# Scores, pooled scores and values by head: two row halves of the matrix engine, two banks, no zero blocks, and a new issue order

## The chip, the cores and the metric

The kernel runs on one core of a Trainium2 chip. The metric is the device time of one execution in microseconds. The core's engines are PE (TensorE: matmuls, and PEld for the loads of their stationary weights), DVE (VectorE), ACT (ScalarE), POOL (GpSimd) and SP (SyncE, which issues most DMAs here). Each has its own instruction queue and works through it in order; semaphores tie them together. SBUF is the working memory of 128 partitions, PSUM the memory of eight banks (128 partitions by 512 f32 each) into which PE writes.

## The reference, cut to what matters

Eight batches of eight heads, 576 tokens, 64 numbers a head. The attention has two parts that are added: a local one, in which each token sees the three before and the three behind it, and a pooled one, in which groups of four tokens are averaged (144 rows), attend to each other, and are repeated four times. A mixture of eight experts, one for each token, follows on the 4608 token rows.

```python
q_d = q.reshape(B, H, Sd, factor, D).mean(axis=3)      # k_d, v_d alike; factor 4
out_up = np.repeat(sm_attn(q_d, k_d, v_d), factor, axis=2)
mask = np.abs(pos[:, None] - pos[None, :]) < factor
scores = np.where(mask, scale * np.matmul(q, k.transpose(0, 1, 3, 2)), -1000000000.0)
...
out_local = np.matmul(attn, v)
x = (out_up + out_local).transpose(0, 2, 1, 3).reshape(B * S, H * D)
e_idx = np.argmax(x[do_compute] @ w_gate, axis=1)      # do_compute: x @ w_skip > 0
y[mask] = gate_w[mask, None] * (np.maximum(xc[mask] @ w1[e], 0.0) @ w2[e])
```

## The kernel before, in words

The attention comes first, then the experts. Attention works on 36 tiles of 128 tokens. A tile is four groups of 32 tokens (`QG`); a group's local attention looks at a window of 38 keys (`KW`). Heads go in four pairs. Q and K of a batch lie with the 64 numbers of both heads of a pair on the 128 partitions, heads interleaved (partitions 0, 2, 4 ... are the first head's, 1, 3, 5 ... the second's).

K (`KB`) has two blocks of columns, one for each head, and in the block of a head the other head's partitions are zero. So one matmul over 128 rows gives the scores of both heads of a pair beside each other. For the first two batches K comes with its zeros from memory (`load_kb`); later batches overwrite only the head's own partitions (`load_k`). The pooled K (`KD`, by `pool_k`) keeps that form, and so do the V windows (`VB`, by `load_v`, two DMAs of 48 rows a tile): 96 rows, interleaved by head, with zeros where row and block belong to different heads.

For a tile, `scores` writes the mask by an identity matmul in bf16, then 16 f32 matmuls (four pairs by four groups; a group's 32 tokens are one 32-column strip of the array, and of the partitions of the result). `s_max`, `s_sub`, `s_sum` (DVE), `s_exp` (ACT) and `norm` (POOL) make the probabilities `E`; `p_transpose` turns them through PE, `p_evac` copies them out of PSUM; `up_mm` starts the result `O` with the pooled attention repeated by a matmul with a 0/1 matrix (`rep`); `values` adds 16 f32 matmuls; `x_out` copies `O` to `X`, `store_x` writes it, and `x_transpose`, `x_evac`, `logits` prepare the routing. For a batch, `d_scores` (five a batch), `d_max`, `d_neg`, `d_exp`, `d_transpose`, `d_values`, `d_out`, `d_hi`, `d_lo` make the pooled attention `up` in a high and a low half. Routing (`route`) runs every eight tiles.

PSUM is in four pools of two banks each: `psS` for scores, `psD` for pooled scores and routing, `psT` for what is transposed, `psO` for results and logits.

The order on every engine is not the program's own: all steps are recorded as nodes, and the table `ORDER` (1262 numbers) says in which order they are issued on all engines and queues. Each engine then runs its part in order and waits for what its next instruction needs: data, or the release of a buffer of a pool.

The lines by which a step can be found in the profile of before: L252 and L249 `d_scores`, L241 `pool_k`, L257, L262, L273 the maximum, negation and exponential of pooled scores, L306 to L318 `d_values`, L335 `d_out`, L341 and L344 `d_hi` and `d_lo`, L352 the mask, L357 the scores, L362, L368, L374, L378 the softmax steps, L394 `p_transpose`, L398 `p_evac`, L413 `up_mm`, L419 `values`, L424 `x_out`, L433 `x_transpose`, L445 `logits`, L825 and L845 the two matmuls of the experts.

Of the kernel before, what the change touches and what calls it, by code (L numbers as in the profile page):

```python
# [108 lines left out]
)  # L109

@with_exitstack
def tile_attention_moe(ctx, tc, qT, kT, kB, vW, v4, vr, mask, cst, ups, cid, w9, w1, w2, out):
# [77 lines left out]
    def load_v(i):  # L193
        V = TT[i]["VB"] = VBs[i % 3]
        for r in range(2):
            nc.sync.dma_start(out=V[r::2, r].rearrange("p a g d -> p (a g d)"), in_=vW[i, r])
# [839 lines left out]
```

## Time and profile before

| | us |
|---|---|
| median of 3 runs (lowest to highest) | 506.4 (503.98 to 508.02) |
| the profiled execution's own time | 505.92 |
| its span, from first to last instruction | 504.1 |
| PE busy | 447.2 (89%) |
| PE weight loads busy | 381.8 (76%) |
| DVE busy | 316.3 (63%) |
| ACT busy | 242.8 (48%) |
| POOL busy | 167.8 (33%) |
| DMA | 101.50 MB, mean 201 GB/s |

Busy is the union of an engine's instructions, and the ends of matmuls are modelled, so how long PE is held by a piece of work is better read from the distance between starts. A row of grouped instructions has line, engine, operation, tiles (out<-in), shapes and count; behind the bar its busy time, the mean of one in ns, and the idle time of the engine just before, with what ended it. A row of the timeline has start, length, then the same and a count. A row of waits has who waited for whom, in total, how often, and the longest.

### The profile page before, as it was taken

What the parts mean: (1) busy time and instruction counts of PE and PEld (TensorE: products, weight loads), DVE (VectorE), ACT (ScalarE), POOL (GpSimd) and SP (SyncE); (2) the same over time, 40 slices, a digit from 0 to 9 for tenths busy, and PEclk for the clock granted to TensorE, in tenths of its full rate; (3) what the DMA queues carried; (4) which work ended last, traced back from release to release, by engine and by line L of the source; (5) the groups of instructions that cost most, each with busy time, mean ns of one, the idle gap of its engine ahead of it and who ended that gap; (6) DMA issues with size and microseconds to landing.
All of it is one profiled execution on the core that took longest, in us unless ns stands there. A gap on an engine that the chain in (4) does not pass through costs nothing. (4 is left out here: it accounts for less than half of the span.)

```text
span 504.1 us, 13771 instructions
## 1 busy us (share of the span) xinstructions
PE 447.2 (89%) x5642; PEld 381.8 (76%) x5642; DVE 316.3 (63%) x617; ACT 242.8 (48%) x558; POOL 167.8 (33%) x178
## 2 busy tenths in 40 slices
PE   0678899989997999998499999999999999999991
PEld 0346677767886778886389898989989889898981
DVE  1799689479967995625254655635676755567421
ACT  1356477637683677462244354335454534454310
POOL 7356667465736352110420040410505050201002
PEclk9999989999999999998589999999999999999996
DMA  7986996989899663451554555464666753555201
GB/s 271 356 282 194 304 340 212 305 275 312 233 303 338 213 199 108 158 164 60 181 177 126 169 194 168 136 225 134 231 218 238 238 190 121 177 192 169 84 4 56
DMA packets 34620, 101.50 MB, mean 201 GB/s; under 512 B 5069, under 2 KB 6349, under 8 KB 34530
## 3 DMA queue, kind: packets, MB, share of 16 engines
q1 hardware_dynamic: 30690, 89.14, 53.7%
q0 software_dynamic: 3840, 11.09, 6.2%
q8 instruction: 65, 1.06, 0.9%
q14 instruction: 25, 0.20, 0.1%
HBM read 85.98 MB, written 15.73 MB: 202 GB/s over the span
## 5 line engine op out<-in xcount | busy, mean ns | idle before, releaser
L794 POOL DMA_INDIRECT out<-Y,six x24 | 24.2, 1009 | 192.6 <-DVE Y L852 189.7
L825 PE MATMUL ph<-xth,w1h 128*128 128x384 f32 (+2 forms) x256 | 81.6, 319 | 0.7 <-issue 0.7
L825 PE MATMUL ph<-xtl,w1h 128*128 128x384 f32 (+2 forms) x256 | 79.8, 312 | 0.1
L825 PE MATMUL ph<-xth,w1l 128*128 128x384 f32 (+2 forms) x256 | 79.7, 311 | 0.0
L845 PE MATMUL py<-w2h,hh 128*128 128x512 f32 x168 | 65.8, 392 | 0.5
L845 PE MATMUL py<-w2l,hh 128*128 128x512 f32 x168 | 65.8, 392 | 0.0
L845 PE MATMUL py<-w2h,hl 128*128 128x512 f32 x168 | 65.6, 391 | 0.0
L834 ACT ACTIVATE hh<-ph 128x384 fp32r<-128x384 f32 x64 | 31.3, 491 | 58.3 <-PE ph L825 28.2
L835 DVE SCALAR_TENSOR_TENSOR hl<-ph,hh 128x384 fp32r<-128x384 f32 x64 | 34.7, 554 | 37.5 <-ACT hh L834 35.8
L825 PEld LDWEIGHTS ph<-xth,w1h 128*128 128x128 f32 x256 | 49.1, 192 | 1.5 <-issue 1.1
L825 PEld LDWEIGHTS ph<-xtl,w1h 128*128 128x128 f32 x256 | 49.0, 191 | 0.8 <-issue 0.4
L241 DVE TENSOR_REDUCE KD<-KB 128x288 f32<-128x1152 f32 x31 | 40.8, 1339 | 13.7 <-DMA KB<-kB 11.5
L825 PEld LDWEIGHTS ph<-xth,w1l 128*128 128x128 f32 x256 | 48.9, 191 | 0.0
L387 POOL TENSOR_TENSOR Et<-Et,r 128x304 f32<-128x304 f32 x36 | 25.9, 725 | 62.7 <-DVE r L384 36.6
L599 DVE TENSOR_TENSOR w2l<-raw,w2h 128x1024 fp32r<-128x1024 f32 x32 | 39.1, 1221 | 10.7 <-ACT w2h L598 10.5
L614 DVE TENSOR_TENSOR w1l<-raw,w1h 128x1024 fp32r<-128x1024 f32 x32 | 39.2, 1224 | 9.4 <-ACT w1h L609 9.4
L816 ACT CAST xth<-Tx 128x512 fp32r<-128x512 f32 x22 | 12.9, 587 | 62.7 <-PE Tx L813 59.3
L252 PE MATMUL Sd<-KD,qd 128*128 128x288 f32 x64 | 23.9, 470 | 19.2 <-DVE KD L241 16.6
L817 DVE TENSOR_TENSOR xtl<-Tx,xth 128x512 fp32r<-128x512 f32 x22 | 15.2, 692 | 40.5 <-ACT xth L816 37.2
L598 ACT CAST w2h<-raw 128x1024 fp32r<-128x1024 f32 x32 | 33.6, 1050 | 14.4 <-PE py L845 14.4
L419 PE MATMUL O<-VB,PT 96*32 96x128 f32 x1152 | 38.3, 274 | 0.0
L794 POOL DMA_INDIRECT xr<-out,gix x24 | 27.7, 1154 | 30.9 <-DMA raw<-w 23.8
(136 smaller groups left out, 962.4 us busy)
## 6 DMA issues: line engine op xcount, KB each, us to landing
raw<-w SPq DMA_DIRECT2D x64, 512.0 KB, 3.3
VB<-vW SPq DMA_DIRECT2D x72, 192.0 KB, 4.6
out<-X SPq DMA_DIRECT2D x36, 256.0 KB, 3.7
V<-v SPq DMA_DIRECT2D x16, 512.0 KB, 9.4
Q<-qT SPq DMA_DIRECT2D x7, 1152.0 KB, 8.8
KB<-kT SPq DMA_DIRECT2D x12, 576.0 KB, 9.3
KB<-kB SPq DMA_DIRECT2D x4, 832.0 KB, 7.1
KB<-kB SPq DMA_DIRECT2D x2, 768.0 KB
```

The lines of the kernel that those rows point to most:

```text
L241: nc.vector.tensor_reduce(out=kd, in_=kv, axis=AX.X, op=ALU.add)
L252: nc.tensor.matmul(pairs(S), lhsT=B[b]["qd"][:, n, :128], rhs=kd[:, :, n, :], start=True, stop=True)
L387: nc.gpsimd.tensor_tensor(out=TT[i]["E"], in0=TT[i]["E"], in1=heads(TT[i]["r"])[:, :, None, :].to_broadcast([128, 4, KW, 2]), op=ALU.mult)
L419: nc.tensor.matmul(O[quad[j], 128 * a:128 * a + 128], lhsT=PT[:, a, quad[j]], rhs=VB[:, :, a, j, :], start=False, stop=a == 3)
L598: nc.scalar.copy(out=hf, in_=raw)
L599: nc.vector.tensor_tensor(out=flat(lo), in0=raw, in1=hf.bitcast(F32), op=ALU.subtract)
L614: nc.vector.tensor_tensor(out=flat(lo), in0=raws[e, j], in1=flat(hi).bitcast(F32), op=ALU.subtract)
L794: ins = nc.gpsimd.indirect_dma_start(bounds_check=NOUT - 1, oob_is_err=False, **kw).ins
L825: nc.tensor.matmul(P[i][:, :n], lhsT=a[:, c, 128 * i:128 * i + 128], rhs=bb[:, c, :n], start=m == 0, stop=m == 11)
L834: nc.scalar.activation(out=hh[:, i], in_=p, func=AF.Relu)
L835: nc.vector.scalar_tensor_tensor(out=hl[:, i], in0=p, scalar=0.0, in1=hh[:, i].bitcast(F32), op0=ALU.max, op1=ALU.subtract)
L845: nc.tensor.matmul(py[k], lhsT=a[:, i, ks], rhs=bb[:, i, :], start=(j == 0 and i == 0 and m == 0), stop=(j == 3 and i == 1 and m == 2))
```

## The change

Each head is now worked by itself over its own rows. Q, K and their pooled forms have a pair's first head on partitions 0 to 63 and the second on 64 to 127; the zero blocks and the loads of them are gone (`KB` and `KD` are half as wide, and only three columns at each end of K are filled with zeros). A pair's two heads are two matmuls, one in each row half of the array, and their results go to two PSUM banks: `scores` has 32 f32 matmuls of 38 columns in place of 16 of 76 (and eight of the mask for four), `d_scores` two of 144 for one of 288, `values` 32 of 64 columns for 16 of 128. `values` takes 38 of each 64 rows; `KR` goes from 48 to 64, so a V window has 128 rows, is loaded by one DMA, and has four buffers in place of three.

PSUM: a tile of `psS` is two banks and is shared by scores, pooled scores and routing (two buffers); `psO` is one buffer of two banks, for results alone; `d_values` and `logits` take a buffer of `psT`. `up_mm` writes each 512-column step as two of 256; for the last 64 tokens of a batch it has one step for both halves of `up`, where it had four of 128 columns, and for that `d_out` spreads the rest rows over 512 columns (`d_spread_r`, and `up` is 1024 wide, before 640).

```diff
-KR = 48
+KR = 64
-NREP = R_REST + 4 * 192
+NREP = R_REST + 192
...
     psS = pool(att, "psS", 2, space=PSUM)
-    psD = pool(att, "psD", 2, space=PSUM)
     psT = pool(att, "psT", 2, space=PSUM)
-    psO = pool(att, "psO", 2, space=PSUM)
+    psO = pool(att, "psO", 1, space=PSUM)
...
-    KBs = [kvp.tile([128, 2, KF], F32, name=f"KB{i}") for i in range(2)]
-    VBs = [kvp.tile([WV, 2, 4, 4, HD], F32, name=f"VB{i}") for i in range(3)]
-    Es = [kvp.tile([128, 4, KR, 2], F32, name=f"Et{i}") for i in range(3)]
+    KBs = [kvp.tile([128, KF], F32, name=f"KB{i}") for i in range(2)]
+    VBs = [kvp.tile([WV, 4, 4, HD], F32, name=f"VB{i}") for i in range(4)]
+    Es = [kvp.tile([128, H, KR], F32, name=f"Et{i}") for i in range(3)]
...
-    halves = [slice(0, 128, 2), slice(1, 128, 2)]
+    halves = [slice(0, 64), slice(64, 128)]
...
-        V = TT[i]["VB"] = VBs[i % 3]
-        for r in range(2):
-            nc.sync.dma_start(out=V[r::2, r].rearrange("p a g d -> p (a g d)"), in_=vW[i, r])
+        V = TT[i]["VB"] = VBs[i % 4]
+        nc.sync.dma_start(out=V.rearrange("p a g d -> p (a g d)"), in_=vW[i])
...
     def pool_k(b, p):
-        kd, o = KDs[b % 2][:, :, p, :], KO + SEQ * p
-        kv = KBs[b % 2][:, :, o:o + SEQ].rearrange("p h (i r) -> p h i r", r=4)
-        if b == 0 and p == 1:
-            for r in range(3):
-                nc.gpsimd.tensor_add(out=kd, in0=kv[:, :, :, 0] if r == 0 else kd, in1=kv[:, :, :, r + 1])
-        else:
-            nc.vector.tensor_reduce(out=kd, in_=kv, axis=AX.X, op=ALU.add)
+        kd, o = KDs[b % 2][:, p, :], KO + SEQ * p
+        kv = KBs[b % 2][:, o:o + SEQ].rearrange("p (i r) -> p i r", r=4)
+        nc.vector.tensor_reduce(out=kd, in_=kv, axis=AX.X, op=ALU.add)
...
     def d_scores(b, n):
-        S = psD.tile([128, 512], F32, name="Sd")
...
-            nc.tensor.matmul(pairs(S), lhsT=B[b]["qd"][:, n, :128], rhs=kd[:, :, n, :], start=True, stop=True)
...
+        S = psS.tile([128, 2, 512], F32, name="S")
+        Sv, kd, qd = S[:, :, :SD], KDs[b % 2], B[b]["qd"]
+        for p in range(4) if n == 4 else (n,):
+            rows, q = (quad[p], slice(SD - 32, SD)) if n == 4 else (slice(None), slice(0, 128))
+            for h, hs in enumerate(halves):
+                nc.tensor.matmul(Sv[rows, h], lhsT=qd[hs, p, q], rhs=kd[hs, p], start=True, stop=True)
...
+    def d_spread_r(b):
+        r = B[b]["rm"] = smp.tile([128, 4, 2], F32, name="rm", bufs=2)
+        nc.vector.tensor_tensor(out=r, in0=B[b]["rd", 1][:, None, :].to_broadcast([128, 4, 2]),
+                                in1=cs[:, C_SP4:C_SP4 + 4][:, :, None].to_broadcast([128, 4, 2]), op=ALU.mult)
...
         for p in range(4):
             for j, b, g in groups(i):
                 o, k = SEQ * p + QG * g, KO + SEQ * p + QG * g - 3
-                nc.tensor.matmul(Sv[quad[j], 2 * p:2 * p + 2], lhsT=B[b]["Q"][:, o:o + QG],
-                                 rhs=KBs[b % 2][:, :, k:k + KW], start=False, stop=p == 3)
+                for h, hs in enumerate(halves):
+                    nc.tensor.matmul(Sv[quad[j], h, p], lhsT=B[b]["Q"][hs, o:o + QG], rhs=KBs[b % 2][hs, k:k + KW],
+                                     start=False, stop=p == 3)
...
     def up_mm(i):
-        O = TT[i]["O"] = psO.tile([128, 512], F32, name="O")
...
+        for n, (l, u) in enumerate(steps):
+            for h in range(2):
+                nc.tensor.matmul(O[:, h], lhsT=l, rhs=u.rearrange("p (a h d) -> p h a d", a=4, h=2)[:, h],
+                                 start=n == 0, stop=False)
...
         for a in range(4):
             for j in range(4):
-                nc.tensor.matmul(O[quad[j], 128 * a:128 * a + 128], lhsT=PT[:, a, quad[j]], rhs=VB[:, :, a, j, :],
-                                 start=False, stop=a == 3)
+                for h in range(2):
+                    rows = slice(KR * h, KR * h + KW)
+                    nc.tensor.matmul(O[quad[j], h, a], lhsT=PT[rows, a, quad[j]], rhs=VB[rows, a, j],
+                                     start=False, stop=a == 3)
...
-        Lp = LP[i0] = psO.tile([128, 512], F32, name="O")
+        Lp = LP[i0] = psT.tile([128, 512], F32, name="T")
```

`ORDER` is a new table. On PE, at the first tiles, before (L413 is `up_mm`, L419 `values`, L252 a pooled score, L433 and L394 the transposes; the numbers tell buffers of one name apart):

```order
L413 MATMUL O_487<-upH_470,rep_120 128x512
L413 MATMUL O_487<-upL_471,rep_120 128x512
L413 MATMUL O_490<-upH_470,rep_120 128x512
L413 MATMUL O_490<-upL_471,rep_120 128x512
L419 MATMUL O_487<-VB0_114,PT_474 32x128 x16
L252 MATMUL Sd_519<-KD1_122,qd_455 128x288
L433 MATMUL T_522<-ident_69,X_517 128x128 x4
```

The same place with the change (L421 is `values`, L412 `up_mm`, L435 the x transpose, L239 a pooled score):

```order
L421 MATMUL O_607<-VB0_111,PT_553 32x64 x32
L412 MATMUL O_708<-upH_543,rep_118 128x256 x2
L412 MATMUL O_708<-upL_544,rep_118 128x256 x2
L435 MATMUL T_717<-ident_69,X_700 128x128 x4
L239 MATMUL S_724<-KD1_120,qd_533 128x144 x2
L239 MATMUL S_732<-KD1_120,qd_533 128x144 x2
L421 MATMUL O_708<-VB1_112,PT_557 32x64 x32
```

Two results were begun ahead of the first `values`; now the second `up_mm` stands behind the first `values`, with nothing between them, and can only start once `O_607` is copied out.

On PE around the tiles 7 and 8, before (the second `values` is tile 8's; it is also one of the tiles with last rows of a batch, hence the matmuls of 128 columns):

```order
L419 MATMUL O_1363<-VB1_115,PT_1182 32x128 x16
L433 MATMUL T_1425<-ident_69,X_1311 128x128 x4
L394 MATMUL T_1436<-ident_69,Et0_117 96x128 x4
L413 MATMUL O_1445<-upH_938,rep_120 128x512
L413 MATMUL O_1445<-upL_939,rep_120 128x512
L413 MATMUL O_1445<-upH_938,rep_120 128x128 x4
L413 MATMUL O_1445<-upL_939,rep_120 128x128 x4
L433 MATMUL T_1463<-ident_69,X_1430 128x128 x4
L419 MATMUL O_1445<-VB2_116,PT_1270 32x128 x16
```

With the change, around the tiles 8 and 9 (L392 is `p_transpose`):

```order
L421 MATMUL O_1806<-VB0_111,PT_1788 32x64 x32
L392 MATMUL T_1900<-ident_69,Et1_116 128x128 x4
L435 MATMUL T_1909<-ident_69,X_1795 128x128 x4
L412 MATMUL O_1916<-upH_1741,rep_118 128x256 x2
L412 MATMUL O_1916<-upL_1742,rep_118 128x256 x2
L435 MATMUL T_1927<-ident_69,X_1905 128x128 x4
L239 MATMUL S_1935<-KD1_120,qd_1751 128x144 x2
L421 MATMUL O_1916<-VB1_112,PT_1815 32x64 x32
L239 MATMUL S_1978<-KD1_120,qd_1751 128x144 x2
```

Between a tile's `values` and the next `up_mm` stand a transpose of probabilities and one of x, as before. The pooled scores of a batch now stand close to each other between the steps of the tiles, and take the buffers `S` that the scores take too.

More of the change, by code (lines that the diff above doesn't have):

```diff
@@ L41, with tile_attention_moe @@
 R_REST = 64 + SEQ
-NREP = R_REST + 4 * 192
+NREP = R_REST + 192
 BIG = float(1 << 20)
 ORDER = (
[61 rows of a table removed]
[61 rows of a table added]
 )
 @with_exitstack
-def tile_attention_moe(ctx, tc, qT, kT, kB, vW, v4, vr, mask, cst, ups, cid, w9, w1, w2, out):
+def tile_attention_moe(ctx, tc, qT, kT, vW, v4, vr, mask, cst, ups, cid, w9, w1, w2, out):
     nc = tc.nc
@@ L154, in tile_attention_moe @@
     ones = kvp.tile([128, 128], BF16, name="ones")
-    KBs = [kvp.tile([128, 2, KF], F32, name=f"KB{i}") for i in range(2)]
-    VBs = [kvp.tile([WV, 2, 4, 4, HD], F32, name=f"VB{i}") for i in range(3)]
-    Es = [kvp.tile([128, 4, KR, 2], F32, name=f"Et{i}") for i in range(3)]
+    KBs = [kvp.tile([128, KF], F32, name=f"KB{i}") for i in range(2)]
+    VBs = [kvp.tile([WV, 4, 4, HD], F32, name=f"VB{i}") for i in range(4)]
+    Es = [kvp.tile([128, H, KR], F32, name=f"Et{i}") for i in range(3)]
     rep = kvp.tile([128, NREP], F32R, name="rep")
-    KDs = [kvp.tile([128, 2, 4, SD], F32, name=f"KD{i}") for i in range(2)]
-    halves = [slice(0, 128, 2), slice(1, 128, 2)]
+    KDs = [kvp.tile([128, 4, SD], F32, name=f"KD{i}") for i in range(2)]
+    halves = [slice(0, 64), slice(64, 128)]
     flat = lambda a: a.rearrange("p a b -> p (a b)")
@@ L175, in load_q, with load_k @@
         nc.sync.dma_start(out=chunk(B[b]["Q"])[:, c], in_=qT[b, c].rearrange("c p n -> p c n"))
[L177 to L183 removed]
+    def load_k(b, c=slice(None)):
+        nc.sync.dma_start(out=chunk(KBs[b % 2][:, KO:KO + 4 * SEQ])[:, c], in_=kT[b, c].rearrange("c p n -> p c n"))
     def load_v4(b, k):
@@ L234, in pool_k @@
     def pool_k(b, p):
-        kd, o = KDs[b % 2][:, :, p, :], KO + SEQ * p
-        kv = KBs[b % 2][:, :, o:o + SEQ].rearrange("p h (i r) -> p h i r", r=4)
-        if b == 0 and p == 1:
-            for r in range(3):
-                nc.gpsimd.tensor_add(out=kd, in0=kv[:, :, :, 0] if r == 0 else kd, in1=kv[:, :, :, r + 1])
-        else:
-            nc.vector.tensor_reduce(out=kd, in_=kv, axis=AX.X, op=ALU.add)
-    def d_scores(b, n):
-        S = psD.tile([128, 512], F32, name="Sd")
-        pairs = lambda rows: rows[:, :2 * SD].rearrange("p (a k) -> p a k", a=2)
-        kd = KDs[b % 2]
-        if n == 4:
-            for p in range(4):
-                nc.tensor.matmul(pairs(S[32 * p:32 * p + 32]), lhsT=B[b]["qd"][:, p, SD - 32:], rhs=kd[:, :, p, :],
-                                 start=True, stop=True)
-        else:
-            nc.tensor.matmul(pairs(S), lhsT=B[b]["qd"][:, n, :128], rhs=kd[:, :, n, :], start=True, stop=True)
-        B[b]["Sd"][n] = pairs(S)
+        kd, o = KDs[b % 2][:, p, :], KO + SEQ * p
+        kv = KBs[b % 2][:, o:o + SEQ].rearrange("p (i r) -> p i r", r=4)
+        nc.vector.tensor_reduce(out=kd, in_=kv, axis=AX.X, op=ALU.add)
+    def d_scores(b, n):
+        S = psS.tile([128, 2, 512], F32, name="S")
[4 more added lines that the diff above has]
+                nc.tensor.matmul(Sv[rows, h], lhsT=qd[hs, p, q], rhs=kd[hs, p], start=True, stop=True)
+        B[b]["Sd"][n] = Sv
     def d_max(b, n):
@@ L301, in d_values @@
         s = B[b]
-        O = psO.tile([128, 512], F32, name="O")
+        O = psT.tile([128, 512], F32, name="T")
         PT, vd = s["PTd"], s["vd"]
@@ L334, in d_out @@
-        upS = s["upS"][:, D:] if c else s["upS"][:, :D]
-        nc.vector.scalar_tensor_tensor(out=upS.rearrange("p (h d) -> p h d", h=n),
-                                       in0=s["Od", c][:, :n * HD].rearrange("p (h d) -> p h d", h=n), scalar=0.25,
-                                       in1=s["rd", c][:, :, None].to_broadcast([128, n, HD]), op0=ALU.mult, op1=ALU.mult)
+            s["upS"] = dp.tile([128, 2, D], F32, name="upS", bufs=1)
+        if c == 0:
+            hd = lambda a: a.rearrange("p (h d) -> p h d", h=H)
+            o, r = hd(s["Od", 0]), s["rd", 0][:, :, None].to_broadcast([128, H, HD])
+        else:
+            hd = lambda a: a.rearrange("p (a h d) -> p a h d", a=4, h=2)
+            o = s["Od", 1][:, :128].rearrange("p (h d) -> p h d", h=2)[:, None].to_broadcast([128, 4, 2, HD])
+            r = s["rm"][:, :, :, None].to_broadcast([128, 4, 2, HD])
@@ L339, in d_hi @@
+        nc.vector.scalar_tensor_tensor(out=hd(s["upS"][:, c]), in0=o, scalar=0.25, in1=r, op0=ALU.mult, op1=ALU.mult)
     def d_hi(b):
-        B[b]["up"] = [dp.tile([128, D + 128], F32R, name="upH"), dp.tile([128, D + 128], F32R, name="upL")]
-        nc.scalar.copy(out=B[b]["up"][0], in_=B[b]["upS"])
+        B[b]["up"] = [dp.tile([128, 2, D], F32R, name="upH"), dp.tile([128, 2, D], F32R, name="upL")]
+        nc.scalar.copy(out=flat(B[b]["up"][0]), in_=flat(B[b]["upS"]))
     def d_lo(b):
-        nc.vector.tensor_tensor(out=B[b]["up"][1], in0=B[b]["upS"], in1=B[b]["up"][0].bitcast(F32), op=ALU.subtract)
+        nc.vector.tensor_tensor(out=flat(B[b]["up"][1]), in0=flat(B[b]["upS"]), in1=flat(B[b]["up"][0]).bitcast(F32),
+                                op=ALU.subtract)
@@ L347, in scores @@
     def scores(i):
-        S = psS.tile([128, 512], F32, name="S")
-        Sv = TT[i]["S"] = S[:, :H * KW].rearrange("p (h k) -> p h k", h=H)
+        S = psS.tile([128, 2, 512], F32, name="S")
+        Sv = TT[i]["S"] = S[:, :, :4 * KW].rearrange("p h (a k) -> p h a k", a=4)
         for j, b, g in groups(i):
             v = 0 if g == 0 else (2 if g == NG - 1 else 1)
-            nc.tensor.matmul(Sv[quad[j]], lhsT=idb[:, quad[j]], rhs=mk[:, v:v + 1, :].to_broadcast([128, H, KW]),
-                             start=True, stop=False)
+            for h, hs in enumerate(halves):
+                o = 64 * h + 32 * (j % 2)
+                nc.tensor.matmul(Sv[quad[j], h], lhsT=idb[hs, o:o + 32], rhs=mk[hs, v:v + 1, :].to_broadcast([64, 4, KW]),
+                                 start=True, stop=False)
@@ L401, in up_mm @@
     def up_mm(i):
-        O = TT[i]["O"] = psO.tile([128, 512], F32, name="O")
-        main, rest = [], []
+        O = psO.tile([128, 2, 512], F32, name="O")
+        O = TT[i]["O"] = O[:, :, :4 * HD].rearrange("p h (a d) -> p h a d", a=4)
+        steps = []
         for b in sorted({b for j, b, g in groups(i)}):
             o = 128 * i - SEQ * b
-            if o < 4 * 128:
-                main += [(O, rep[:, 64 + o:192 + o], u[:, :D]) for u in B[b]["up"]]
-            if o + 128 > 4 * 128:
-                r = R_REST + o - 448
-                rest += [(O[:, 128 * p:128 * p + 128], rep[:, r + 192 * p:r + 192 * p + 128], u[:, D:])
-                         for u in B[b]["up"] for p in range(4)]
-        for n, (o, l, u) in enumerate(main + rest):
-            nc.tensor.matmul(o, lhsT=l, rhs=u, start=n == 0, stop=False)
+            for u in B[b]["up"]:
+                if o < 4 * 128:
+                    steps.append((rep[:, 64 + o:192 + o], u[:, 0]))
+                if o + 128 > 4 * 128:
+                    steps.append((rep[:, R_REST + o - 448:R_REST + o - 320], u[:, 1]))
+        for n, (l, u) in enumerate(steps):
+            for h in range(2):
+                nc.tensor.matmul(O[:, h], lhsT=l, rhs=u.rearrange("p (a h d) -> p h a d", a=4, h=2)[:, h],
+                                 start=n == 0, stop=False)
     def values(i):
@@ L468, in bank @@
         def bank(name):
-            R[name] = psD.tile([128, 512], F32, name="Sd")
+            R[name] = psS.tile([128, 2, 512], F32, name="S")[:, 0]
             return R[name]
@@ L636, in load_zrow @@
     def load_zrow():
-        nc.sync.dma_start(out=out[0:1, :], in_=VBs[0][0:1, 1, :2].rearrange("p a g d -> p (a g d)"))
+        nc.sync.dma_start(out=out[0:1, :], in_=flat(Es[2])[0:1])
     node(load, mkf, mask)
@@ L642, in tile_attention_moe @@
         node(load_q, 0, slice(c, c + 1))
-        node(load_kb, 0, c)
+        node(load_k, 0, slice(c, c + 1))
+    for i in range(2):
+        for o in (KO - 3, KO + 4 * SEQ):
+            node(fill, nc.vector, KBs[i][:, o:o + 3])
     node(copy, nc.vector, idb, ident)
     node(copy, nc.vector, mk, mkf)
-    node(fill, nc.gpsimd, VBs[0])
     node(fill, nc.gpsimd, Es[0])
@@ L649, in tile_attention_moe @@
     node(load, cs, cst)
-    reps = slice(0, R_REST), slice(R_REST, NREP)
-    repf = [rawp.tile([128, 1024], F32, name="raw")[:, :c.stop - c.start] for c in reps]
-    for r, c in enumerate(reps):
-        node(load, repf[r], ups[:, c])
+    repf = rawp.tile([128, 1024], F32, name="raw")[:, :NREP]
+    node(load, repf, ups)
     for j in range(2):
@@ L659, in tile_attention_moe @@
     node(load, w9t, w9)
+    for i in range(1, 3):
+        node(fill, nc.gpsimd, Es[i])
     node(load_zrow)
-    for i in range(1, 3):
-        node(fill, nc.gpsimd, VBs[i])
-        node(fill, nc.gpsimd, Es[i])
     node(fill, nc.gpsimd, ones, 1.0)
     node(copy, nc.vector, tri, cs[:, C_TRI:C_TRI + 128])
-    for r, c in enumerate(reps):
-        node(copy, nc.scalar, rep[:, c], repf[r])
+    node(copy, nc.scalar, rep, repf)
     node(copy, nc.vector, BT, cs[:, C_BASE:C_BASE + E + 1])
@@ L671, in tile_attention_moe @@
             node(load_q, b)
-            for c in range(3) if b == 1 else ():
-                node(load_kb, b, c)
-            for hh in range(2) if b > 1 else ():
-                node(load_k, b, hh)
+            node(load_k, b)
             for j in range(3):
@@ L972, in layouts @@
     f32 = np.float32
-    pair = lambda a: np.ascontiguousarray(a.reshape(B, 4, 2, SEQ, HD).transpose(0, 4, 2, 1, 3)).reshape(B, 128, 4, SEQ)
+    pair = lambda a: np.ascontiguousarray(a.reshape(B, 4, 2, SEQ, HD).transpose(0, 2, 4, 1, 3)).reshape(B, 128, 4, SEQ)
     chunks = lambda a: np.ascontiguousarray(a.reshape(B, 128, 3, CH).transpose(0, 2, 1, 3))
     qT, kT = chunks(pair(q)), chunks(pair(k))
-    kB = np.zeros((2, 128, 2, KF), f32)
-    for h in range(2):
-        kB[:, h::2, h, KO:KO + 4 * SEQ] = pair(k)[:2, h::2].reshape(2, 64, 4 * SEQ)
     vp = np.zeros((B, H, QG * (NG - 1) + KR, HD), f32)
@@ L1011, in layouts @@
     ups[:, :R_REST] = tok[None] // 4 == row[:, None]
-    for p in range(4):
-        for t in range(64):
-            ups[32 * p + 16 + t // 4, R_REST + 192 * p + 64 + t] = 1.0
+    for t in range(64):
+        ups[16 + t // 4::32, R_REST + 64 + t] = 1.0
     w9 = np.concatenate([moe_w_gate, moe_w_skip[:, None]], axis=1)
@@ L1021, in layouts @@
     w2 = np.ascontiguousarray(w2).reshape(E, 4, 128, 1024)
-    return dict(qT=qT, kT=kT, kB=kB, vW=vW, v4=v4, vr=vr, mask=mask, cst=cst, ups=ups, cid=cid, w9=w9, w1=w1, w2=w2)
+    return dict(qT=qT, kT=kT, vW=vW, v4=v4, vr=vr, mask=mask, cst=cst, ups=ups, cid=cid, w9=w9, w1=w1, w2=w2)
 def kernel(q, k, v, moe_w_skip, moe_w_gate, moe_w1, moe_w2):
```

35 lines of the change are left out of this document (14 added, 21 removed), and 122 rows, old and new, of the table ORDER.

## The prediction

> **What bounds the kernel now.** I first split the span into stages, with each engine's busy time, the share of the DMA engines that was busy, and GB/s.
>
> ```profile
> core 0: us, PE busy (x) PEld busy (x) DVE busy (x) ACT busy (x) POOL busy (x), PEclk, DMA share, GB/s
> 0.00:16.60 16.60, 0.00 (x0) 0.03 (x1) 3.71 (x4) 1.28 (x1) 10.32 (x21) 1.00 0.84 302
> 16.60:50.00 33.40, 27.22 (x522) 18.66 (x522) 30.40 (x66) 19.48 (x68) 18.63 (x22) 1.00 0.81 261
> 50.00:175.00 125.00, 112.61 (x2427) 89.91 (x2424) 99.75 (x231) 77.64 (x236) 72.68 (x71) 0.99 0.88 282
> 175.00:230.00 55.00, 55.00 (x1236) 46.32 (x1239) 32.66 (x95) 35.04 (x94) 14.25 (x19) 1.00 0.48 159
> 242.00:504.00 262.00, 243.90 (x1371) 219.58 (x1371) 141.27 (x178) 106.63 (x155) 51.90 (x48) 0.96 0.49 165
> ```
>
> The attention fills the first 230 us, then comes a routing tail to 242 and the expert half, which the change doesn't touch: those 262 us stay. Before 16.6 PE waits for data; up to 50 VectorE is the fullest (30.4 of 33.4); from 50 to 175 PE leads (112.6 of 125), with DMA close behind (0.88); from 175 to 230 PE has no gap at all. So a shorter PE pays whole only at the end. The start:
>
> ```profile
> 15.10 1.35 DVE L241 TENSOR_REDUCE KD<-KB 128x288 f32<-128x1152 f32 x1 [11.54 <-DMA KB<-kB]
> ```
>
> The first K must land (15.1) and be pooled before PE has work. Next, PE in one piece of its timeline (start, length, records; a new group's start ends the turn of the one before):
>
> ```profile
> 130.89 0.32 PE L352 MATMUL S<-mk,idb 128*32 128x304 bf16 x4
> 131.03 0.70 PE L357 MATMUL S<-KB,Q 128*32 128x76 f32 x32
> 131.56 1.05 PE L419 MATMUL O<-VB,PT 96*32 96x128 f32 x32
> 132.44 1.03 PE L306 MATMUL O<-vb,PTd 128*32 128x512 f32 x8
> 133.30 1.06 PE L309 MATMUL O<-vd,PTd 128*32 128x64 f32 x64
> 134.19 0.39 PE L313 MATMUL O<-vb,PTd 128*32 128x128 f32 x8
> 134.73 1.24 PE L252 MATMUL Sd<-KD,qd 128*128 128x288 f32 x4
> 135.81 0.38 PE L394 MATMUL T<-ident,Et 128*96 128x128 f32 x2
> ```
>
> Mask, scores and values of a tile hold PE for 0.14, 0.53 and 0.88 us; two pooled scores for 1.08. Each f32 matmul leaves two records. L309 starts 64 records in 0.89 us, one per 13.9 ns, though one of 64 columns lasts far longer: the four 32-column strips of the array already work side by side. What the change adds is two row halves side by side, which no row shows.
>
> **PE, worked out.** If the halves overlap fully, each of these turns halves: scores 0.26 x 36 = 9.5 us, mask 0.07 x 36 = 2.5, values 0.44 x 36 = 15.8, pooled scores 0.25 x 40 = 10 (the fifth of a batch, in strips, counted alike). The upsampling of a batch's last rows:
>
> ```profile
> 227.29 0.39 PE L413 MATMUL O<-upH,rep 128*128 128x512 f32 x1
> 227.53 0.39 PE L413 MATMUL O<-upL,rep 128*128 128x512 f32 x1
> 227.76 0.56 PE L413 MATMUL O<-upH,rep 128*128 128x128 f32 x4
> 228.15 0.61 PE L413 MATMUL O<-upL,rep 128*128 128x128 f32 x4
> 228.69 1.96 PE L419 MATMUL O<-VB,PT 96*32 96x128 f32 x64
> ```
>
> Two matmuls of 512 columns take 0.47, eight of 128 take 0.93: short ones cost 0.116 each, though a quarter of 0.235 is 0.06, and I read the difference as the load of 128 weight columns. Four of 256 should take 0.47, so 0.46 x 8 = 3.7 less; a main step split in two stays at 0.47. Sum: 41 us less of PE's 195 up to 230. The other end: if starts come no closer than 13.9 ns, 64 records of scores take 0.89 instead of 0.53 (+13 us), values stay, pooled scores gain nothing (four loads of 0.116 are 0.46), so PE gets 9 us longer. I take the 41, since L309's strips, the nearest row, do run together, and the two banks keep the halves' results apart; both ends stay in the range.
>
> By the Trainium skill ("TensorEngine Tiling (Array Packing)", Theoretical Speedup), a contraction of up to 64 rows can gain up to 2x, which gives the same 41 us; no row here shows it. A rule that speaks against the change stands in "TensorE: Matmul & The Clock Gate" (Wait — 56ns, not 53.3ns?): starts never come closer than about 25 ns, however few the columns. By it scores and values would take 1.6 us each, some 65 us more in all; L309's 13.9 ns per record disagrees, at least across strips, so I give it no chance beside that of the no-overlap rival below.
>
> **VectorE, ScalarE, GpSimd.**
>
> ```profile
> L241 DVE TENSOR_REDUCE KD<-KB 128x288 f32<-128x1152 f32 x31 | 40.8, 1339 | 13.7 <-DMA KB<-kB 11.5 <-DMA KB<-kT 2.1
> L257 DVE TENSOR_REDUCE nmd<-Sd 128x2 f32<-128x288 f32 x40 | 17.7, 444 | 4.5 <-PE Sd L252 4.5
> L335 DVE SCALAR_TENSOR_TENSOR upS<-O,rd 128x512 f32<-128x512 f32 x8 | 5.5, 685 | 2.7 <-PE O L309 2.5
> L335 DVE SCALAR_TENSOR_TENSOR upS<-O,rd 128x128 f32<-128x128 f32 x8 | 2.3, 281 | 3.1 <-PE O L318 3.1
> L344 DVE TENSOR_TENSOR upL<-upS,upH 128x640 fp32r<-128x640 f32 x8 | 8.3, 1032 | 0.2
> L341 ACT CAST upH<-upS 128x640 fp32r<-128x640 f32 x8 | 5.8, 727 | 10.2 <-DVE upS L335 10.1
> L424 ACT COPY X<-O 128x512 f32<-128x512 f32 x36 | 21.0, 588 | 22.7 <-PE O L419 21.8 <-DMA VB<-vW 0.9
> ```
>
> Pooling K halves to 576 elements; on the line between 444 ns at 288 and 1339 at 1152 that is 742: 31 x 0.60 = 18.5 less. Added: the 32nd, which leaves GpSimd (0.7), 8 x 0.40 for the wider second upS (3.2), 8 x 0.2 for the spread reciprocal (1.6; eight elements, so under the 281 ns of the narrow upS), upL from 640 to 1024 columns (between 0 and 0.62 each; I take 3). VectorE ends 10 us shorter, ScalarE about 3 longer (upH). GpSimd loses its K adds and VB fills, all ahead of the first work. The KB fills of three columns fall into VectorE's first 11.54 us of idling. Maximum, subtraction and sum keep their 304 elements in another pattern, which I set at nothing; L335's 685 ns for 512 elements and 444 for L257's 288 (1.34 and 1.54 ns each) bound it at some 13% of 108 passes of 0.47, 6 us either way, beside a fuller DMA. The probability transposes load 128 columns for 96: between nothing and 144 x 32 x 0.116/128 = 4 us of PE; nothing, since PE loads the next weights while it works.
>
> **DMA.**
>
> ```profile
> KB<-kB SPq DMA_DIRECT2D x4, 832.0 KB, 7.1
> KB<-kB SPq DMA_DIRECT2D x2, 768.0 KB
> VB<-vW SPq DMA_DIRECT2D x72, 192.0 KB, 4.6
> ```
>
> V windows grow from 2 x 192 to 512 KB a tile: +4.6 MB. K of batches 0 and 1 shrinks from 2432 to 1152 KB each: -2.6 MB, and the ups table loses 288 KB. Net +1.8 MB, but 1.28 MB less ahead of the first matmul. SP issues each V window once, not twice, and has four VB buffers:
>
> ```profile
> SPq L196 <- PE O L419: 31.7, 17, 6.3
> ```
>
> So far SP stood 31.7 us at V loads until the values three tiles before were done, with all later loads and stores behind it. A fourth buffer takes most of that, and what is late next is the transfer itself: the DMA engines, already at 0.88.
>
> **Waits that are added.** psO has one buffer. PE can start up_mm(i+1) only when X(i) is copied: about 0.6 (L424) plus some 0.3 for the last matmul's end. In the new order mostly one or two transposes or scores stand between (a scores turn is 0.53 now), twice nothing; queued behind are values and all later PE work. I count 0.15 x 36 = 5 us, of which PE's slack hides half: +2. Pooled scores, scores and routing now share two S buffers instead of four. A pooled S is held for matmul, maximum, negation and two exps:
>
> ```profile
> L262 ACT ACTIVATE nmd<-nmd 128x2 f32<-128x2 f32 x40 | 8.1, 202 | 32.5 <-DVE nmd L257 32.5
> L273 ACT ACTIVATE Ed<-Sd,nmd 128x144 f32<-128x144 f32 x80 | 29.7, 377 | 0.9
> L273 ACT ACTIVATION_READ_ACCUMULATOR Ed<-Sd,nmd 128x1 f32 x80 | 15.9, 199 | 0.0
> L368 DVE TENSOR_TENSOR Et<-S,nm 128x304 f32<-128x304 f32 x36 | 16.7, 467 | 4.9 <-PE T L394 4.3
> ```
>
> 0.5 + 0.44 (L257) + 0.20 + 2 x 0.58 = 2.3 us; a tile's S for its turn and two passes of 0.47, 1.5. A batch has 5 and 4.5 of them: 18 us on two buffers, 9 of a batch's 27 us (230 - 16.6 over 8). A third of the time, so I take nothing, and price it below. The pooled values (1.8 us with L306 and L309, then a upS pass of 0.69) and the logits move onto the transposes' two T buffers: at most 5 us a batch there, over two, which I set at nothing too. PE also waits for nothing the profile shows:
>
> ```profile
> PE O L309 <- issue: 2.4, 1, 2.4
> PE O L318 <- issue: 2.4, 1, 2.4
> PE T L394 <- issue: 2.4, 2, 1.9
> PE S L357 <- issue: 1.8, 2, 1.2
> ```
>
> 9 us over some 4200 records up to 230. If that goes with the count of instructions, the 2600 records added (32 x 36 each for scores and values, 4 x 36 of the mask, some 130 of pooled scores) make 6 more, a third of it on the path: +2.
>
> **The sum by stage.** Start: 1.28 MB at 302 GB/s, -4. To 50: seven pooled Ks of 0.6, -3. From 50 to 175: PE falls to 89 (41 x 113/195 less), VectorE to 94 (10 x 125/213 less), but DMA stood at 110 and gets about 2.8 MB more (22 tiles), 8 us at 282/0.88 = 320 GB/s; its 118 becomes the bound, -6. From 175 on: PE's backlog, which is 55 us of unbroken work, loses a fifth, 11, and one more since PE follows the loads closer, -12. Together -25; waits +4, and 2 for a coarse split: -19. From the profiled execution's 505.9 (span 504.1 and 1.8 around it; the median is 506.4) that gives **487**.
>
> **Rivals.**
> *Nothing but PE counts*: DMA sustains more than 320 GB/s. For it: the start moved 302 GB/s at a share of 0.84, which is 360 at full share. Against it: the fullest 25 us, at a share over 1, gave 325.
>
> ```profile
> 50.00:75.00 25.00, 22.57 (x465) 17.05 (x466) 18.80 (x39) 14.47 (x50) 16.32 (x15) 0.93 1.03 325
> ```
>
> Then stage three gives 14 and the tail 19: **466**.
> *The halves don't overlap* (the change doesn't do what it says): PE stays or gets up to 9 longer; start and VectorE still give 7, waits cost 4, PE +5: **508**.
> *The shared S buffers decide* (slower): PE stands at a pooled score or a score until the S two before it is read. There are 76 such; the net gain of 19 is gone at 0.25 us each on the path. For it: the new order puts several pooled scores within 2 us of PE work, against 2.3 us of holding, and their readers queue in order on VectorE and ScalarE. Against it: the third computed above. At 0.4 us each, 30 us: **517**.
>
> **How the numbers follow.** Forecast 0.58 (475 to 497 by itself), only-PE 0.16, no overlap 0.15, S buffers 0.11. Range 465 to 510: out stay half of the 466 case, some of 508 and most of 517. A measurement tells about 1% from no change, so faster means below 501: 0.58 + 0.16 + 0.03 of the no-overlap case = 0.77; within 1% 0.11; slower 0.12.
>
> **What would show it.** Right: values turn 0.44 us and scores 0.27 on PE's timeline; the first matmul near 12 us; PE's busy share between 50 and 175 below 0.8 with DMA above 0.93; expert half still 262. Wrong: turns of 0.88 (no overlap); PE waits named ACT Ed or DVE Et before S matmuls, or ACT X before up_mm, that sum to over 15 us; a batch period of 27 us with neither PE nor DMA full.

## The result: slower, 558.8 us against 505.2

The changed kernel takes 558.84 us (median of four, 557.31 to 562.57), the kernel before beside it 505.19 (501.03 to 508.02): 1.108 times, with an interval of 1.098 to 1.118. The forecast was 487. The profiled execution took 557.78 us (span 556.0).

First the stages of the changed kernel, in the same columns as in the prediction:

```profile
core 0: us, PE busy (x) PEld busy (x) DVE busy (x) ACT busy (x) POOL busy (x), PEclk, DMA share, GB/s
0.00:16.60 16.60, 6.01 (x108) 3.92 (x108) 10.33 (x26) 6.20 (x20) 5.80 (x19) 1.00 0.88 319
16.60:50.00 33.40, 25.18 (x720) 20.05 (x719) 19.32 (x49) 13.03 (x40) 17.25 (x18) 0.70 0.74 278
50.00:175.00 125.00, 100.62 (x3047) 82.61 (x3052) 77.71 (x176) 65.44 (x198) 54.83 (x55) 0.82 0.65 221
175.00:230.00 55.00, 42.68 (x1454) 36.10 (x1449) 30.57 (x82) 26.30 (x71) 20.05 (x21) 0.88 0.67 229
230.00:293.00 63.00, 50.48 (x1593) 42.10 (x1580) 32.94 (x123) 29.30 (x76) 7.41 (x12) 0.97 0.27 91
```

From 50 us on nothing is full: PE 100.6 of 125, DMA at 0.65, and in the last 63 us PE still has gaps with DMA at 0.27. The granted clock is down to 0.70 and 0.82, where it was 1.00 and 0.99. All the loss lies in the attention; the first matmul of the expert half, in the timelines of before and of after:

```profile
247.68 1.11 PE L813 MATMUL Tx<-ident,xr 128*128 128x128 f32 x4 [5.09 <-DMA xr<-out,gix]
```

```profile
298.64 1.09 PE L812 MATMUL Tx<-ident,xr 128*128 128x128 f32 x4 [5.14 <-DMA xr<-out,gix]
```

It starts 51 us later, and what follows takes as long as before (257.4 us, before 256.4). Up to these two moments PE was busy, before and after (one window each):

```profile
0.00:247.68 247.68, 203.92 (x4275) 162.65 (x4275) 175.66 (x443) 138.71 (x408) 118.88 (x133) 0.97 0.74 241
```

```profile
0.00:298.64 298.64, 225.46 (x6891) 185.15 (x6891) 171.53 (x456) 142.81 (x407) 108.40 (x127) 0.85 0.60 207
```

So of the 51 us, 21.5 are more busy time of PE (225.5 - 203.9) and 29.4 more idle time (73.2 against 43.8), although the start is 9.7 us earlier (before, the first matmul came at 16.60):

```profile
6.91 0.85 PE L239 MATMUL S<-KD,qd 64*128 64x144 f32 x4 [6.91 <-POOL qd L218]
```

PE's waits in that window say what fills the gaps (waiter, what it waited for, us in total, times, longest):

```profile
PE S L357 <- issue: 20.6, 12, 4.8
PE O L421 <- issue: 10.2, 6, 3.5
...
PE T L296 <- issue: 5.3, 2, 3.6
...
PE S L351 <- ACT Ed L260: 2.3, 2, 1.6
...
PE O L412 <- ACT X L426: 1.9, 2, 1.2
```

"issue" is time in which PE waited for nothing that the profile shows. With the smaller rows of the same name it is 44.2 us, against 9.2 before. The last two rows are the shared buffers, which the slower rival had in mind: a few us. The turns themselves, in two stretches of the timeline without a pause, where the granted clock was full:

```profile
193.78 0.26 PE L351 MATMUL S<-mk,idb 64*32 64x152 bf16 x8
193.86 0.76 PE L357 MATMUL S<-KB,Q 64*32 64x38 f32 x64
194.46 0.85 PE L421 MATMUL O<-VB,PT 38*32 38x64 f32 x64
195.24 0.66 PE L392 MATMUL T<-ident,Et 128*128 128x128 f32 x4
...
244.08 0.52 PE L239 MATMUL S<-KD,qd 64*128 64x144 f32 x4
244.53 0.86 PE L421 MATMUL O<-VB,PT 38*32 38x64 f32 x64
```

From start to start: values 0.78 us (0.88 before, 0.44 forecast), scores 0.60 (0.53 before, 0.27 forecast), a pooled score 0.45 (0.54, 0.25), the mask 0.08 (0.14, 0.07). What comes next also counts: with a transpose behind it a scores turn takes 0.69 (0.64 before), and values 0.79 (0.98 before). And one of the stalls, in the middle of one `values`:

```profile
185.85 0.78 PE L421 MATMUL O<-VB,PT 38*32 38x64 f32 x54
190.08 0.34 PE L421 MATMUL O<-VB,PT 38*32 38x64 f32 x5 [3.45 <-issue]
```

54 of 64 records run, all operands of the rest are there, and PE stands 3.45 us. From the page, the whole program and the queue that carries instructions (packets, MB, share):

```profile
span 556.0 us, 18958 instructions
PE 469.8 (84%) x8258; PEld 405.1 (73%) x8258; DVE 312.1 (56%) x630; ACT 247.0 (44%) x557; POOL 156.6 (28%) x172
q8 instruction: 86, 1.41, 1.0%
```

Before it was 65 packets with 1.06 MB for 13771 instructions and 5642 matmul records. A packet is 16.4 KB; 21 more of them came for 5187 more instructions, about 250 in each. A matmul record has a weight load beside it, so a packet holds about 128 such pairs.

The trace also holds when each packet of that queue starts. Up to the expert half it is 54 packets for PE's 6891 records, one for 128, and no two of them start less than 3.2 us apart. The 16 "issue" stalls of over 1 us come 127 or 128 records apart or, to within a few records, a multiple of that, and each ends 2.2 to 2.6 us after a packet has begun.

### The profile page after: what moved, and what is told of

It reads as the page before. It is cut to its first block, busy times and chain, and to the rows that moved or that the text cites. A ratio compares the mean times of both kernels' runs of the same rounds, so it can differ in the third digit from the quotient of the medians.

```text
span 556.0 us, 18958 instructions
## 1 busy us (share of the span) xinstructions
PE 469.8 (84%) x8258; PEld 405.1 (73%) x8258; DVE 312.1 (56%) x630; ACT 247.0 (44%) x557; POOL 156.6 (28%) x172
## 5 line engine op out<-in xcount | busy, mean ns | idle before, releaser
L357 PE MATMUL S<-KB,Q 64*32 64x38 f32 x2304 | 32.6, 225 | 20.7 <-issue 20.6
L357 PEld LDWEIGHTS S<-KB,Q 64*32 64x32 f32 x2304 | 28.1, 119 | 22.5 <-issue 22.3
L421 PE MATMUL O<-VB,PT 38*32 38x64 f32 x2304 | 35.2, 239 | 10.2 <-issue 10.2
L421 PEld LDWEIGHTS O<-VB,PT 38*32 38x32 f32 x2304 | 28.2, 113 | 16.2 <-issue 14.5
L362 DVE TENSOR_REDUCE nm<-S 128x8 f32<-128x304 f32 x36 | 16.9, 469 | 37.7 <-PE S L357 37.5
```

Of the source, the lines that this page charges most:

```text
L357: nc.tensor.matmul(Sv[quad[j], h, p], lhsT=B[b]["Q"][hs, o:o + QG], rhs=KBs[b % 2][hs, k:k + KW], start=False, stop=p == 3)
L362: nc.vector.tensor_reduce(out=pairs(nm), in_=TT[i]["S"], axis=AX.X, op=ALU.max)
L421: nc.tensor.matmul(O[quad[j], h, a], lhsT=PT[rows, a, quad[j]], rhs=VB[rows, a, j], start=False, stop=a == 3)
```

## Experiments

Two theories were put against each other. **I**: PE doesn't get its instructions fast enough, because each head is now a matmul of its own. **W**: the shared PSUM buffers and the new order. Then how many us a record costs, and what else the change holds.

**split_both**: the kernel before, with each f32 matmul of scores and values cut into two of half the columns. Order, pools, data and zero blocks stay; 2304 more records.

```diff
-                nc.tensor.matmul(Sv[quad[j], 2 * p:2 * p + 2], lhsT=B[b]["Q"][:, o:o + QG],
-                                 rhs=KBs[b % 2][:, :, k:k + KW], start=False, stop=p == 3)
+                for h in range(2):
+                    nc.tensor.matmul(Sv[quad[j], 2 * p + h], lhsT=B[b]["Q"][:, o:o + QG],
+                                     rhs=KBs[b % 2][:, h, k:k + KW], start=False, stop=p == 3 and h == 1)
...
```

> The kernel before with each scores matmul of 76 columns split into two of 38 (still over 128 rows with the zero blocks) and each values matmul of 128 columns into two of 64: the same columns stream, in the old order and with the old PSUM pools, but PE gets 2304 more matmul records. Theory I (PE can't get its instructions fast enough): 535 to 565 us, with PE's idle time put down to issue up from 9 to over 30 us. Theory W (the shared PSUM buffers and the new order cost the time): 503 to 510 us.

553.67 us, 1.102 (1.095 to 1.110). The count alone brings 47 us, nearly the whole slow-down, with the old order, the old pools and no row halves. PE's waits, and its window up to the first matmul of the expert half (at 293.43):

```profile
PE S L358 <- issue: 22.5, 13, 3.8
...
PE O L421 <- issue: 8.4, 7, 2.8
```

```profile
0.00:293.43 293.43, 223.19 (x6578) 182.35 (x6578) 176.64 (x443) 139.88 (x408) 118.54 (x133) 0.93 0.63 204
50.00:175.00 125.00, 99.93 (x2963) 81.14 (x2965) 79.69 (x183) 64.65 (x201) 61.12 (x60) 0.92 0.71 230
```

Busy +19.3, idle +26.5, "issue" 39.3 in all: nearly the same account as that of the change. Its scores turn, without row halves and with a transpose behind it, is 0.79:

```profile
145.91 0.86 PE L358 MATMUL S<-KB,Q 128*32 128x38 f32 x64
146.70 0.64 PE L395 MATMUL T<-ident,Et 128*96 128x128 f32 x4
```

The same 64 records with row halves take 0.69, so short matmuls do gain from the halves, but less than the split costs (0.64 before).

**split_scores**: only the scores cut that way, 1152 more records.

> The kernel before with the scores matmuls alone split into two of 38 columns: 1152 records more instead of 2304. Theory I, with a price by record as in the run that split both (47 us for 2304): 525 to 536 us. If the cost is a step that comes once PE has too much of them: at 505 or at 550.

528.89 us, 1.042 (1.035 to 1.049): half the records, a little under half the loss.

**after_half**: the changed kernel with one matmul for a pair instead of two, over all 128 rows into the first bank, for scores and values. It leaves half of the heads' scores and values out; order, pools and buffers are those of the change, with 2304 records fewer.

```diff
-                for h, hs in enumerate(halves):
-                    nc.tensor.matmul(Sv[quad[j], h, p], lhsT=B[b]["Q"][hs, o:o + QG], rhs=KBs[b % 2][hs, k:k + KW],
-                                     start=False, stop=p == 3)
+                nc.tensor.matmul(Sv[quad[j], 0, p], lhsT=B[b]["Q"][:, o:o + QG], rhs=KBs[b % 2][:, k:k + KW],
+                                 start=False, stop=p == 3)
...
```

> The changed kernel, where scores and values work only one matmul for a pair, over all 128 rows into the first bank (so half the heads get no scores and no local values): the order, the PSUM pools and all else stay, PE has 2304 records fewer, as many as before the change. Theory I: 480 to 515 us. Theory W: 540 to 560 us.

502.98 us, 0.995 (0.990 to 1.000). With the count back at 5954, order, sharing and new layout stand, and the slow-down is gone.

```profile
50.00:175.00 125.00, 103.56 (x2516) 81.97 (x2508) 91.22 (x219) 71.80 (x207) 64.28 (x66) 0.92 0.80 278
```

The granted clock of this stage is 0.92, as in split_both (0.93 in both up to the expert half), though the two are 51 us apart: the clock is not what sets them apart. This is not a version to keep, since it does half of the work in these two steps; split_both has no such gap and points the same way.

**after_half_values**: the same for values alone, 1152 records fewer than the change.

> The changed kernel, where only values works one matmul for a pair, over 128 rows into the first bank (half the heads get no local values): 1152 records fewer. Theory I with the same price each as between the changed kernel and the run that left out both halves (56 us for 2304): 525 to 537 us.

531.75 us, 1.053 (1.045 to 1.061), in the middle between after_half and the change. The price of a record, each against its neighbour:

| step | records | us | ns each |
|---|---|---|---|
| before to split_scores | +1152 | +22.2 | 19 |
| before to split_both | +2304 | +47.0 | 20 |
| after_half to after_half_values | +1152 | +28.8 | 25 |
| after_half to the change | +2304 | +55.9 | 24 |

Such a price holds what the record adds to its turn, to the stalls and to the work at a low clock.

**pace**: PE by itself. Of the computation nothing is left: one block of Q is loaded, PE runs 256 f32 matmuls of 76 columns in four strips (L29), 512 of 38 columns by row halves into two banks (L36) and 128 of 304 columns likewise (L43); the stores come after that.

> PE alone, with next to no DMA: 256 f32 matmuls in four strips over 128 rows with 76 columns, then 512 by head over 64 rows with 38 columns, then 128 by head with 304 columns, on the same small tile; nothing of the reference is computed. If the halves overlap: eight records of 304 columns in some 0.26 us; else in 0.51. If PE's own pace bounds short ones: records of 38 columns come every 11 to 17 ns rather than the 4 ns of the streaming, with a pause at each 128 records if instructions come in blocks of 16 KB that are fetched late; without such pauses, the pauses in the kernel come from the data's DMAs.

The timeline of PE:

```profile
10.74 3.74 PE L29 MATMUL Bb<-q 128*32 128x76 f32 x211
15.51 2.31 PE L29 MATMUL Bb<-q 128*32 128x76 f32 x128 [1.03 <-issue]
19.24 2.31 PE L29 MATMUL Bb<-q 128*32 128x76 f32 x128 [1.42 <-issue]
22.96 0.99 PE L29 MATMUL Bb<-q 128*32 128x76 f32 x45 [1.42 <-issue]
...
34.70 1.61 PE L36 MATMUL A<-q 64*32 64x38 f32 x128 [2.11 <-issue]
38.43 1.61 PE L36 MATMUL A<-q 64*32 64x38 f32 x128 [2.11 <-issue]
42.16 1.61 PE L36 MATMUL A<-q 64*32 64x38 f32 x128 [2.12 <-issue]
```

128 records, a pause, 128 records, a pause: every 3.73 us one block, whether a block's work takes 2.31 us or 1.61. The first pause comes only after 223 records (12 at the start and these 211). That is 29 ns a record with DMA next to idle, and the block is a packet of the instruction queue: each pause ends 2.3 to 2.9 us after a packet has begun. Windows of pace (its columns have no ACT): the strips with their first pauses, the short by-head matmuls, then two of the 304-column ones.

```profile
core 0: us, PE busy (x) PEld busy (x) DVE busy (x) POOL busy (x), PEclk, DMA share, GB/s
15.50:23.90 8.40, 5.56 (x304) 5.12 (x303) 0.00 (x0) 0.00 (x0) 1.00 0.02 4
23.90:53.30 29.40, 12.57 (x1029) 11.51 (x1030) 0.24 (x1) 0.00 (x0) 0.56 0.02 4
53.30:58.30 5.00, 5.00 (x93) 2.88 (x96) 0.24 (x1) 0.00 (x0) 0.50 0.02 7
58.30:64.00 5.70, 5.70 (x184) 3.49 (x168) 0.00 (x0) 0.00 (x0) 1.00 0.01 3
```

Two more things stand here. The granted clock is still 1.00 with the first pauses, falls to 0.56 on the mean in the stretch that follows, and is 1.00 again after 5 us without a pause, while a block comes every 3.73 us at either clock. So the pauses don't come from the low clock; that they bring it along is what this order in time suggests. And the row halves do overlap: at full clock a 304-column record takes 5.70/184 = 31 ns. Four strips without halves took 0.86 us for eight records of 512 columns (L306 in the prediction's rows), which is 64 ns for 304 columns. The halves bring a factor of two where a record is long enough.

By the Trainium skill ("Runtime: NRT & Kernel Launch", Instruction fetch mechanics), instructions come in blocks of 16 KiB, 256 instructions, and the fetch is hidden behind the rate at which they are issued. The size agrees with 16.4 KB a packet; that it is hidden does not hold for PE here, with 2.11 us of every 3.73 idle.

**after_no_v**: the change without the V loads after the first four tiles, to see whether data transfers slow the supply. Later tiles work on old V, so other tokens go to other experts, and only the attention part can be read.

> The changed kernel without the loads of the V windows after the first four tiles (later tiles use old windows): 16.8 MB less traffic, the same instructions on PE. Theory I with the fetch of instructions slowed by the data's DMAs: PE's issue idle falls from 44 us to under 25, 520 to 545 us. Theory I with PE's own pace alone: the issue idle stays near 44, 550 to 560 us. Theory W: 545 to 560 us.

765.42 us in all, which isn't comparable. The expert half begins at 293.02 (298.64 in the change), "issue" is 40.4 us (44.2), and the DMA share between 50 and 175 us is 0.48 (0.65). The supply is short with or without these 16.8 MB.

**old_mm_new_order**: the matmuls of before in the order and pools of the change.

> The kernel before with its own matmuls, zero blocks and loads, but issued in the order of the changed kernel and with its PSUM sharing: scores, pooled scores and routing on two S buffers, one O buffer, pooled values and logits on the T buffers (three V window buffers, since a fourth does not fit). Theory I: 500 to 518 us. Theory W: 540 to 560 us, with PE's or its readers' waits at S and O.

714.45 us, of no use: the V fills came behind V loads, most of V was zero, and the routing was another. It was replaced by the next two.

**old_mm_new_order2** and **old_mm_new_order2_oldps**: the same with the V fills at the start and each V load behind the values that free its buffer (three buffers, as before); the second keeps the four old pools.

```diff
     psS = pool(att, "psS", 2, space=PSUM)
-    psD = pool(att, "psD", 2, space=PSUM)
     psT = pool(att, "psT", 2, space=PSUM)
-    psO = pool(att, "psO", 2, space=PSUM)
+    psO = pool(att, "psO", 1, space=PSUM)
...
```

> The kernel before in the order of the changed one and with its PSUM sharing (S two buffers for three users, one O buffer, T for pooled values and logits), the V fills at the start, and each V load moved behind the values that free its buffer (three buffers here). PE has as many records as before. Theory I alone: 500 to 520 us. If order and buffers cost by themselves, which extra instructions hide: 530 to 560 us.

> The same as the run beside it, but with the four old PSUM pools of two buffers each. If the shared buffers cost: faster than it by 10 us or more. If the order costs (or nothing does): within 5 us of it.

523.7 us, 1.035 (1.030 to 1.041), and 521.94, 1.032 (1.026 to 1.038). Sharing the buffers costs nothing that can be told. The order costs some 3% with the old matmuls and three V buffers: 523.7 fits neither range of its expectation. In after_half, with four V buffers and half of the work, no such loss is to be seen, and split_both is slow in the old order. So W isn't needed for the slow-down; whether the order adds a few us to it in the change isn't settled.

**k_zeroed**: the kernel before with the heads in contiguous row halves, K loaded in halves of 64 partitions, and the zero blocks written by VectorE. It tries for the early start alone.

```diff
-    halves = [slice(0, 128, 2), slice(1, 128, 2)]
+    halves = [slice(0, 64), slice(64, 128)]
...
-        nc.sync.dma_start(out=KBs[b][:, :, cols], in_=kB[b, :, :, cols])
+        for h in range(2):
+            load_k(b, h, slice(c, c + 1))
...
```

> The kernel before with the heads of Q and K on the two contiguous row halves and the zero blocks of K filled by VectorE at the start instead of loaded: 2.6 MB less to load, 1.3 MB of it ahead of the first matmul; matmuls, order and pools as before. Since the changed kernel's first matmul came at 6.9 us and not at 16.6: 496 to 503 us. If the start is not on the path: 505.

523.34 us, 1.027 (1.019 to 1.035): a miss, expected faster. The first matmul starts at 14.45 rather than 16.60, but the transfers got worse. Two windows of k_zeroed, and the second of them in the kernel before:

```profile
16.60:50.00 33.40, 28.67 (x564) 19.56 (x565) 29.34 (x70) 21.38 (x76) 17.28 (x19) 0.95 0.80 219
50.00:100.00 50.00, 42.22 (x879) 33.00 (x878) 33.55 (x75) 28.95 (x92) 31.35 (x30) 0.97 0.94 257
```

```profile
50.00:100.00 50.00, 45.47 (x962) 35.41 (x960) 37.17 (x83) 32.02 (x102) 31.98 (x31) 0.97 0.91 289
```

A fuller DMA moves less: 257 GB/s at 0.94 against 289 at 0.91. From 16.6 to 50 us it is 219 at 0.80, where the kernel before has 261 at 0.81 and the change, with K over all 128 partitions in one DMA (and V loaded in another way too), 278 at 0.74. By the Trainium skill ("SBUF — State Buffer", Door 1: The DMA port swizzle), 64 contiguous partitions reach half of the memory's ports; the rows agree, but no run here measures a single such load. "issue" also doubled, to 19.6 us at the same count of records, so a DMA near full may slow the supply; that wasn't followed up.

**lean** and **after_lean**: fewer records for the same work. Where a tile's four groups share a mask, one mask matmul serves for four (two for eight in the change), and one matmul of `vb` starts all strips at once.

```diff
-            for j in range(4):
-                nc.tensor.matmul(O[quad[j]], lhsT=PT[2][:, 2, quad[j]], rhs=flat(s["vb8"]), start=True, stop=False)
+            nc.tensor.matmul(O, lhsT=PT[2][:, 2], rhs=flat(s["vb8"]), start=True, stop=False)
...
```

> The kernel before with fewer PE instructions for the same numbers: where the four groups of a tile have the same mask, one mask matmul over 128 columns for four in strips, and one matmul for four at the start of each pooled values. Some 170 matmul records fewer of some 4200. Theory I at 20 ns a record: 3 us faster, 501 to 505 where before gives 506. If a record costs only where the other engines leave PE as the bound: no change.

> The changed kernel with the same saving: two mask matmuls for eight where the groups agree, one for four at the start of the pooled values; some 240 records fewer. Theory I at 20 to 24 ns a record: 551 to 555 us. Else 559.

lean: 505.69 us with 168 records fewer, 0.999 (0.995 to 1.003), no change. In its trace "issue" is 5.4 us where the whole program before had 9.9, but PE is busy 5.3 us longer (452.5), so what a record costs at that count isn't settled. after_lean: 549.15 with 240 fewer, 1.089 (1.080 to 1.098), below the change's 1.108, the two intervals just touching; 9.7 us for 240 records is more than the price in the table gives, and below the 551 to 555 expected. No version beats the kernel before.

## Why the prediction was wrong

Two terms of the sum failed: **PE's -41 us, and the +2 for the records added**.

First, the turns. The prediction took scores at 0.27 and values at 0.44, its lower end, "since L309's strips, the nearest row, do run together". That halves overlap was right (pace: 31 ns against 64). But 64 records in 0.27 and 0.44 us would start every 4.2 and 6.9 ns, and in the change they start every 9.4 and 12.2 (0.60 and 0.78 us), between its two ends: short records don't start as fast as their columns would allow. With the turns shown, scores become 36 x 0.07 = 2.5 us longer; shorter become values by 36 x 0.10 = 3.6, the mask by 36 x 0.06 = 2.2, pooled scores by 40 x 0.09 = 3.6 and the last rows of a batch by 8 x 0.34 = 2.7 (1.40 us before, 1.06 now). That is some 10 us less, a quarter of the 41.

Second, the supply. "2600 records added make 6 more, a third on the path: +2" spread the waits of before evenly over its records. They don't go that way: "issue" grew by 35 us, not 6, and the four steps of the table show 19 to 25 ns for every record. In the turns shown the change asks for a record every 9 to 12 ns; pace gets one every 29. What lies between bursts lets the supply catch up (125 us for 3047 records is 41 ns on the mean), but no longer fully. Why it doesn't, when 41 is more than 29, stays open: the traces show when a packet starts, not what it waited for.

The 29.4 us of idle time are the 35 more of "issue" and some 4 of other waits, less the 9.7 of the earlier start. The 21.5 us of busy time are mostly low clock: up to the expert half 71.5 us of PE's busy time lie in stretches of half the clock, 8.4 before. If each record is priced at what those of its line took at full clock, tails beside the stalls included, PE's busy time comes to 203 us, and to 201 before (an estimate from the two traces). Pace shows the low clock following the stalls; no run of the kernel holds the clock fixed, so this division is an account of one trace and not an experiment.

**Start, -4**: right in kind, 9.7 us in fact, and gone by the expert half, which starts 51 us later.

**VectorE, -10**: the pooling was forecast at 742 ns, the wide `upL` between 1032 and 1652:

```profile
L231 DVE TENSOR_REDUCE KD<-KB 128x144 f32<-128x576 f32 x32 | 22.4, 738 | 3.1 <-DMA KB<-kT 3.1
L340 DVE TENSOR_TENSOR upL<-upS,upH 128x1024 fp32r<-128x1024 f32 x8 | 10.5, 1315 | 0.6 <-ACT upH L337 0.4
L319 DVE TENSOR_TENSOR rm<-rd,cs 128x8 f32<-128x8 f32 x8 | 7.6, 954 | 0.2
```

Both hold. Mis-sized is the last row, the spread reciprocal: 954 ns on the mean for eight elements (166 to 1760 for single ones), where 0.2 us had been put because eight are few. So VectorE's busy time falls by 4.2 us (316.3 to 312.1), not 10; with idle time on that engine it decided nothing.

**DMA as the next bound**: wrong. The share is 0.65, not above 0.93: up to the expert half much the same bytes are moved (62 MB, before 60) over 51 us more. SP's first waits show it from the other side:

```profile
SPq L190 <- PE O L421: 138.9, 32, 13.2
```

With a fourth buffer SP stands 138.9 us at V loads, where 31.7 had been with three and less was forecast. In after_half, which isn't slow, it is 85.0 already, so most of that comes with the order and the loads of the change; the rest goes with values that are late themselves. No run tries the buffer alone.

**Waits added, +2, and the S buffers**: right to set them low. ACT X before `up_mm` is 1.9 us, ACT Ed before the mask 2.3, and the old pools gave back 1.8 us (0.3%), less than the runs of one kernel differ.

**The rivals.** No overlap (508) put PE at up to 9 us longer, and was off by less than the forecast of -41, for a wrong reason: the halves do overlap. The 466 of "nothing but PE counts" left out the 4 us of waits, with which its sum is 470. The rule of the Trainium skill that the prediction weighed ("TensorE: Matmul & The Clock Gate", Wait — 56ns, not 53.3ns?), no start within 25 ns of the last, had +65 us. As a floor for starts the rows contradict it (9 to 12 ns). That what a record cost, 19 to 25 ns, and the 53.7 us lost come near to it is luck, since stalls and low clock made them; but a case in which each record costs should have had a chance of its own. None of the signs listed under "Wrong" was "issue"; the row stood in the prediction and was not taken as a bound.
